# Retention and maxout FFN in fp32: the first FFN products by a bilinear algorithm of rank 20

## The chip, the cores and the metric

The kernel runs on one core of one Trainium2 chip. The time is the device time in microseconds; of the kernel before it was taken in three runs, and the median counts. A core has a matrix engine (TensorE, in the profile PE, with its weight loads as a row of their own, PEld), a vector engine (VectorE, DVE), a scalar engine (ScalarE, ACT), GpSimd (POOL) and the queue that starts the DMA transfers (SyncE, SPq). TensorE writes its results to PSUM, which this kernel uses as eight banks; VectorE and ScalarE read them from there. Each engine works through its own list of instructions, and semaphores make one wait for another.

## What is computed

```python
def _attn_ref(q, k, v):                       # 8 batches, 8 heads, 576 positions, 64 per head
    scores = scale * np.matmul(q, k.transpose(0, 1, 3, 2))
    ...
    ret = scores * Dmat[None, :, :, :]        # causal, with a decay per head
    return np.matmul(ret, v)

def _moe_ref(x, w1, w2, w3, w_out):           # x: 4608 tokens x 512, w1..w3: 512 x 768, w_out: 768 x 512
    h = np.maximum(np.maximum(x @ w1, x @ w2), x @ w3)
    return (h @ w_out).astype(np.float32)
```

The output of the attention, with the heads side by side, is the x of the FFN. Everything is in fp32.

## The kernel before

The tokens are worked off in nine tiles of 512 (t = 0 to 8). For each tile the FFN computes the three products with w1, w2, w3 and their maximum h ("up"), and then the product with w_out ("down"). Between the parts of a tile's FFN stand the steps of the attention for the next tile: transposes, scores, masks, states and values; the last of them (`output`) writes the next tile's x. Tile 0 runs plain products, since the weights are still being converted to fp32 then. From tile 1 on, both products are done by a scheme for 2x2 blocks that needs seven block products instead of eight, and sums of blocks ahead and behind.

The pools that matter, and the inputs' sums at the end of `output`:

```python
C = 128; NT = 4 * C; NH = NT // 2
...
    ps_r = ctx.enter_context(tc.tile_pool(name="ps_r", bufs=4, space=PSUM))
    ps_x = ctx.enter_context(tc.tile_pool(name="ps_x", bufs=2, space=PSUM))
    ps_y = ctx.enter_context(tc.tile_pool(name="ps_y", bufs=2, space=PSUM))
...
    def output(chunks, o, t, i):
        ...                                   # xT[t] <- o * decay, on VectorE
        if i == CPT - 1 and t > 0:
            ...
            nc.vector.tensor_tensor(s1[:], a21, a22, op=ALU.add)
            nc.vector.tensor_tensor(s2[:], s1[:], a11, op=ALU.subtract)
            nc.gpsimd.tensor_tensor(s3[:], a11, a21, op=ALU.subtract)
            nc.gpsimd.tensor_tensor(s4[:], a12, s2[:], op=ALU.subtract)
```

One unit of "up" makes two blocks of 128 features of one of the three products; a tile has nine units. A product is two matmuls of 128x128 weights by 256 tokens. Here x, y and z are PSUM banks, and `kept` copies one to SBUF on ScalarE while the chain goes on:

```python
    def up(t, h, fp, i):
        ...
        product(1, x, True)
        p1 = kept("p1", x)
        chore()
        yield
        y = ps_y.tile([P, NH], FP32, tag="y", name="y")
        product(2, y, True)
        nc.vector.tensor_tensor(c11, y[:], p1[:], op=ALU.add)
        yield
        product(6, x, False)
        u2 = kept("u2", x)
        ...
        product(7, z, True)
        p7 = kept("p7", z)
        yield
        product(5, x, False)
        nc.vector.tensor_tensor(c22, x[:], p7[:], op=ALU.add)
        ...
        product(4, z, False)
        nc.vector.tensor_tensor(c21, z[:], u2[:], op=ALU.add)
        if i > 0:
            nc.vector.tensor_tensor(h[:, f1, hi], h[:, f1, hi], c22, op=ALU.max)
        ...
        product(3, x, False)
        ...                                   # two more maxima into h
```

"Down" has seven products of six matmuls each, in the order 1, 2, 6, 7, 5, 4, 3. The step `values` of the attention, and with it `output`, stands between product 7 and product 5:

```python
        product(5, x, False)
        total(1, 1, x, p7)                    # VectorE reads x; product 3 goes into the same bank
        yield
        product(4, z, False)
        total(1, 0, z, u2)
        yield
        ...
            product(3, x, False, blocks)
```

The FFN of a tile and the attention of the next are interleaved so:

```python
    def steps(t):
        ...
        for n in range(0, CPT, 2):
            a, b, m = CPT * t + n, CPT * t + n + 1, 6 * (n // 2)
            at(m, (keep, a), (transposes, a), (load, a + 2))
            at(m + 1, (transposes, b), (decay_values, b))
            at(m + 2, (scores, a), (scores, b), (load, b + 2))
            at(m + 4, (decay_values, a + 2))
            at(m + 5, (values, [a, b], [b, a + 2]))
        return todo

    for t in range(N // NT):
        work = ffn(t)
        for todo in steps(t + 1):
            for step in todo:
                step()
            next(work, None)                  # nine parts of up, then three of down
```

Of the kernel before, what the change touches and what calls it, by code (L numbers as in the profile page):

```python
# [33 lines left out]
FP32 = mybir.dt.float32  # L35
# [7 lines left out]
C = 128  # L43
NT = 4 * C
# [3 lines left out]
FILL = 224  # L48
WAHEAD = 6
# [3 lines left out]
def kernel(  # L53
# [32 lines left out]
    spool = ctx.enter_context(tc.tile_pool(name="spool", bufs=1))  # L86
# [5 lines left out]
    wtmp = while_converting.enter_context(tc.tile_pool(name="wtmp", bufs=4))  # L92
    ps_r = ctx.enter_context(tc.tile_pool(name="ps_r", bufs=4, space=PSUM))
# [28 lines left out]
    def warm_quarters(n):  # L122
        ps = [ps_y.tile([P, P // 2], FP32, tag="y", name="warm") for _ in range(2)]
        for _ in range(n):
            for r in range(2):
                rows = ident[P // 2 * r:P // 2 * (r + 1), :P // 2]
                for c in range(2):
                    nc.tensor.matmul(ps[r][P // 2 * c:P // 2 * (c + 1), :], lhsT=rows, rhs=rows, start=True, stop=True)

# [23 lines left out]
    def load_blocks(g, *blocks):  # L153
        for n, src in (("q", q), ("kx", k)):

            if 0 in blocks:
                raws[n, g] = raw.tile([P, NP, C // 32, 32], FP32, tag=n, name=n + "raw", bufs=3 if n == "q" else 2)
            t = raws[n, g]
            for blk in blocks:
                b, pos = divmod(g * C + 32 * blk, S)  # L160
                for a in range(4):
                    nc.sync.dma_start(
                        t[32 * a:32 * a + 32, :, blk, :],
                        src[b, a // 2::2, pos:pos + 32, 32 * (a % 2):32 * (a % 2) + 32].rearrange("p j i -> j p i"))

    def load(g):
        if g >= BY_PE and ("q", g) not in raws:
            load_blocks(g, *range(C // 32))
        for n, src in (("k", k), ("q", q), ("v", v)) if g < BY_PE else (("k", k), ("v", v)):
            t = raws[n, g] = raw.tile([C, H, D], FP32, tag=n, name=n + "raw", bufs=4 if n == "k" else 3)  # L170
# [110 lines left out]
    def output(chunks, o, t, i):  # L281
# [8 lines left out]
        if i == CPT - 1 and t > 0:  # L290
            x = xT[t]
            a11, a12, a21, a22 = (x[:, 2 * d:2 * d + 2, NH * r:NH * (r + 1)] for r in range(2) for d in range(2))
            s1, s2, s3, s4 = (spool.tile([P, 2, NH], FP32, tag=f"S{n}", name=f"S{n}") for n in (1, 2, 3, 4))
            nc.vector.tensor_tensor(s1[:], a21, a22, op=ALU.add)
            nc.vector.tensor_tensor(s2[:], s1[:], a11, op=ALU.subtract)
            nc.gpsimd.tensor_tensor(s3[:], a11, a21, op=ALU.subtract)
            nc.gpsimd.tensor_tensor(s4[:], a12, s2[:], op=ALU.subtract)
            xS[t] = {1: a11, 2: a12, 3: s4[:], 4: a22, 5: s1[:], 6: s2[:], 7: s3[:]}
# [13 lines left out]
    w_sb, wT, bits, to_load = {}, {}, {}, deque(pieces)  # L312
# [16 lines left out]
    late, chores = {}, deque()  # L329

    def chore(n=1):
        for _ in range(min(n, len(chores))):
            chores.popleft()()
# [21 lines left out]
    def sums_of_hidden(h, fp):  # L355
# [3 lines left out]
        chores.append(lambda: vec(s1, a21, a22, op=ALU.add))  # L359
        chores.append(lambda: vec(s2, s1, a11, op=ALU.subtract))  # L360
        chores.append(lambda: (pool(s3, a11, a21, op=ALU.subtract), pool(s4, a12, s2, op=ALU.subtract)))  # L361

    def downs(t, h):
# [7 lines left out]
        NM = NH // P  # L371
        last = t == N // NT - 1
# [3 lines left out]
        def bank(pool, tag, name):  # L376
            b = pool.tile([P, NM, DM // 2], FP32, tag=tag, name=name)
            return [b[:, m, :] for m in range(NM)]
# [8 lines left out]
        def kept(name, src):  # L387
            both = []
            for m in range(NM):
                c = ppool.tile([P, NH], FP32, tag=name, name=name)  # L390
                nc.scalar.copy(c[:], src[m])
                both.append(c)
            return both
# [5 lines left out]
        def total(r, c, src, others):  # L399
            osb = opool.tile([P, NM, DM // 2], FP32, tag="osb", name="osb")  # L400
            for m, o in enumerate(others):
                nc.vector.tensor_tensor(osb[:, m, :], src[m], o[:], op=ALU.add)
# [7 lines left out]
        p1 = kept("p1", x)  # L410
# [6 lines left out]
        u2 = kept("u2", x)  # L417
# [3 lines left out]
        p7 = kept("p7", z)  # L421
# [15 lines left out]
    def convert_all():  # L437
# [23 lines left out]
        def product(piece, high, expo, mant):  # L461
# [5 lines left out]
            else:  # L467
                w = w_sb[piece] = const.tile([P, DM], FP32, name=f"w{i}_{fb}")[:]
# [13 lines left out]
    def weight_sums(n):  # L482
        if n >= len(units):
            return
        fp, i = units[n]
        half = [slice(0, DM // 2), slice(DM // 2, DM)]
        b11, b21 = (w_sb[i, 2 * fp][:, r] for r in half)
        b12, b22 = (w_sb[i, 2 * fp + 1][:, r] for r in half)
        t1, t2, t4 = (late["pool"].tile([P, DM // 2], FP32, name=f"T{m}_{i}_{fp}")[:] for m in (1, 2, 4))
        nc.vector.tensor_tensor(t1, b12, b11, op=ALU.subtract)  # L490
        nc.vector.tensor_tensor(t2, b22, t1, op=ALU.subtract)
        nc.gpsimd.tensor_tensor(b12, b22, b12, op=ALU.subtract)
        nc.gpsimd.tensor_tensor(t4, b21, t2, op=ALU.subtract)
        wT[fp, i] = {1: b11, 2: b21, 3: b22, 4: t4, 5: t1, 6: t2, 7: b12}
# [7 lines left out]
    def up(t, h, fp, i):  # L502

        f0, f1, lo, hi = 2 * fp, 2 * fp + 1, slice(0, NH), slice(NH, NT)
        x = ps_x.tile([P, NH], FP32, tag="x", name="x")
        y = {}

        def product(n, out, first):
            w = wT[fp, i][n]
            for d in range(2):  # L510
                nc.tensor.matmul(out[:], lhsT=w[:, d * P:(d + 1) * P], rhs=xS[t][n][:, d, :],  # L511
                                 start=first and d == 0, stop=d == 1, skip_group_check=True)

        def kept(name, src):
            c = ppool.tile([P, NH], FP32, tag=name, name=name)
            nc.scalar.copy(c[:], src[:])  # L516
            return c

        if i == 0:
            c11, c21, c22 = h[:, f0, lo], h[:, f0, hi], h[:, f1, hi]  # L520
        else:
            tmp = ppool.tile([P, 3, NH], FP32, tag="tmp", name="tmp", bufs=1)
            c11, c21, c22 = (tmp[:, n, :] for n in range(3))
        product(1, x, True)
        p1 = kept("p1", x)
        chore()
        yield
        y = ps_y.tile([P, NH], FP32, tag="y", name="y")
        product(2, y, True)
        nc.vector.tensor_tensor(c11, y[:], p1[:], op=ALU.add)  # L530
        yield
        product(6, x, False)
        u2 = kept("u2", x)
        chore()
        yield
        z = ps_y.tile([P, NH], FP32, tag="y", name="z")
        product(7, z, True)
        p7 = kept("p7", z)
        yield
        product(5, x, False)  # L540
        nc.vector.tensor_tensor(c22, x[:], p7[:], op=ALU.add)  # L541
        chore()
        yield
        product(4, z, False)
        nc.vector.tensor_tensor(c21, z[:], u2[:], op=ALU.add)
        if i > 0:
            nc.vector.tensor_tensor(h[:, f1, hi], h[:, f1, hi], c22, op=ALU.max)
        yield
        product(3, x, False)
        if i == 0:  # L550
            nc.scalar.copy(h[:, f1, lo], x[:])
        else:
# [203 lines left out]
```

## Time and profile before

| what | value |
|---|---|
| median of three runs | 797.98 us (796.83 to 798.51) |
| span of the profiled run | 796.0 us |
| TensorE, matmul | 785.0 us busy, 5172 instructions |
| VectorE | 417.6 us busy, 833 instructions |
| ScalarE | 174.4 us busy, 402 instructions |
| GpSimd | 139.9 us busy, 158 instructions |
| granted TensorE clock | 1.00 of full speed |

The page of the profile gives for each engine the time in which it worked, then the span in slices, the chain of work that ended last, and groups of instructions by line, engine and shape. One fp32 matmul leaves two records of the matrix engine and two weight loads; so "x4" in a row of the timeline is two matmuls. The ends of matmuls are modelled, so their starts are the better measure. In a row of the timeline stand the start, the duration, the engine, the line, the operation, what it writes and reads, and how long the engine was idle before it and what released it.

By the starts of the "up" matmuls in the timeline, a tile in mid-kernel takes some 85 us: tile 3 from 296.6 to 381.7 us.

### The profile page before, as it was taken

Reading aid. Unit: us, or ns where it says so; the run is one execution under the profiler, and the core shown is the slowest. Engines: PE = TensorE matmul, PEld = TensorE weight load, DVE = VectorE, ACT = ScalarE, POOL = GpSimd, SP = SyncE. Lnnn points to the kernel's source line nnn. Section 1 sums busy time; section 2 is a strip of 40 time slices with the busy share of each in tenths; the row PEclk is TensorE's granted clock in tenths of the full one; section 3 lists DMA queues with packets and bytes.
Section 4 is the critical chain, followed back from the end, with each engine's and each line's share of the span. In section 5 each row is a group of like instructions: output and inputs, shape, how many; then the busy total and the mean of one; then the engine's idle time right before and its main releaser. Section 6 shows DMA issues by size and latency. Waiting matters only on the chain.

```text
span 796.0 us, 13774 instructions
## 1 busy us (share of the span) xinstructions
PE 785.0 (99%) x5172; PEld 643.0 (81%) x5172; DVE 417.6 (52%) x833; ACT 174.4 (22%) x402; POOL 139.9 (18%) x158
## 2 busy tenths in 40 slices
PE   8899999999999999999999999999999999999998
PEld 7445456888888888888888888888888888888887
DVE  2898979664454534364535354544545343642441
ACT  2664632111111111111111111111111111112111
POOL 3110108511210130112111121112111201110000
DMA  9995643333333323332233423333333332001001
GB/s 212 233 230 127 173 91 100 57 55 57 89 58 57 58 75 61 64 58 60 63 56 55 89 59 57 57 57 90 58 55 57 78 68 54 1 14 40 1 1 53
DMA packets 236930, 59.27 MB, mean 74 GB/s; under 512 B 217920, under 2 KB 235584, under 8 KB 236864
## 3 DMA queue, kind: packets, MB, share of 16 engines
q1 hardware_dynamic: 236432, 58.14, 33.9%
q8 instruction: 40, 0.66, 0.4%
q10 hardware_dynamic: 432, 0.27, 0.1%
q14 instruction: 26, 0.21, 0.1%
HBM read 48.89 MB, written 9.44 MB: 73 GB/s over the span
## 4 chain that ended last, share of the span: by engine, by line
PE 95%; SPq 2%; DMA 1%; issue 0%; ACT 0%; DVE 0%; ACTq 0%
PE x L511 32%; PE z L511 15%; PE dx L383 11%; PE up L573 8%; PE y L511 8%; PE dz L383 5%; PE s L204 4%; PE o L257 4%; PE dy L383 3%; PE down L562 2%; PE o L270 2%; PE kv L224 2%; SPq L172 1%; DMA kraw<-in_k_dram 1%; SPq L327 0%; DMA out_dram<-osb 0%
## 5 line engine op out<-in xcount | busy, mean ns | idle before, releaser
L511 PE MATMUL x<-S,T 128*128 128x256 f32 x576 | 148.0, 379 | 0.6 <-ACT p L516 0.6
L511 PEld LDWEIGHTS x<-S,T 128*128 128x128 f32 x576 | 109.0, 190 | 16.4 <-ACT p L516 1.0
L361 POOL TENSOR_TENSOR H<-h 128x256 f32<-128x256 f32 x24 | 21.0, 873 | 320.9 <-DVE h L554 320.9
L511 PE MATMUL x<-xT,w 128*128 128x256 f32 x288 | 76.1, 387 | 0.0
L511 PE MATMUL x<-S,w 128*128 128x256 f32 x288 | 74.4, 381 | 0.7 <-DVE h L541 0.7
L511 PE MATMUL z<-xT,T 128*128 128x256 f32 x288 | 73.9, 379 | 0.0
L511 PE MATMUL y<-xT,w 128*128 128x256 f32 x288 | 73.9, 379 | 0.0
L511 PE MATMUL z<-S,w 128*128 128x256 f32 x288 | 73.9, 379 | 0.0
L541 DVE TENSOR_TENSOR tmp<-x,p 128x256 f32<-128x256 f32 x48 | 20.4, 425 | 100.2 <-PE x L511 100.2
L516 ACT COPY p<-x 128x256 f32<-128x256 f32 x72 | 26.8, 372 | 192.1 <-PE x L511 192.1
L286 DVE TENSOR_TENSOR xT<-o,gq 128x512 f32<-128x512 f32 (+1 forms) x40 | 23.6, 633 | 84.6 <-PE o L270 84.6
L573 PE MATMUL up<-xT,w 128*128 128x512 f32 x144 | 63.5, 596 | 0.5 <-DVE xT L286 0.5
L511 PEld LDWEIGHTS x<-S,w 128*128 128x128 f32 x288 | 49.4, 189 | 14.2 <-issue 1.3
L511 PEld LDWEIGHTS z<-S,w 128*128 128x128 f32 x288 | 54.7, 190 | 7.4
L511 PEld LDWEIGHTS y<-xT,w 128*128 128x128 f32 x288 | 54.7, 190 | 7.4
L511 PEld LDWEIGHTS x<-xT,w 128*128 128x128 f32 x288 | 53.0, 190 | 9.6 <-issue 1.5
L511 PEld LDWEIGHTS z<-xT,T 128*128 128x128 f32 x288 | 54.2, 189 | 7.9
L573 PEld LDWEIGHTS up<-xT,w 128*128 128x128 f32 x144 | 26.8, 190 | 32.3 <-issue 29.8
L207 DVE TENSOR_TENSOR st<-s,causal 128x512 f32<-128x512 f32 x72 | 45.0, 684 | 11.6 <-PE s L204 10.7
L176 POOL TENSOR_TENSOR vd<-vraw,gk 128x512 f32<-128x512 f32 x36 | 38.8, 1077 | 62.1 <-DMA vraw<-in_v_dram 62.1
L516 ACT COPY u<-x 128x256 f32<-128x256 f32 x72 | 26.8, 372 | 100.1 <-PE x L511 91.7
L383 PE MATMUL dx<-To,H 128*128 128x256 f32 x192 | 44.8, 383 | 0.0
(95 smaller groups left out, 1061.8 us busy)
## 6 DMA issues: line engine op xcount, KB each, us to landing
bits<-in_moe_w_dram SPq DMA_DIRECT2D x36, 256.0 KB, 5.1
out_dram<-osb SPq DMA_DIRECT2D x35, 256.0 KB, 2.1
kraw<-in_k_dram SPq DMA_DIRECT2D x32, 256.0 KB, 3.0
vraw<-in_v_dram SPq DMA_DIRECT2D x32, 256.0 KB, 3.5
qraw<-in_q_dram SPq DMA_DIRECT2D x464, 16.0 KB, 1.8
kxraw<-in_k_dram SPq DMA_DIRECT2D x464, 16.0 KB, 1.8
bits<-in_moe_w_out_dram SPq DMA_DIRECT2D x6, 512.0 KB, 4.5
qraw<-in_q_dram SPq DMA_DIRECT2D x6, 256.0 KB, 4.9
```

Source lines behind the costliest of these rows:

```text
L176: nc.gpsimd.tensor_tensor(t[:], raws.pop(("v", g))[:], gk[:].unsqueeze(2).to_broadcast([C, H, D]), op=ALU.mult)
L204: nc.tensor.matmul(s[j][:, p, :], lhsT=kT[r, p, :], rhs=qT[r, p, :], start=True, stop=True)
L207: nc.vector.tensor_tensor(st[:, j], s[j][:], masks[start_of(g)][:].unsqueeze(1).to_broadcast([C, NP, C]), op=ALU.mult)
L224: nc.tensor.matmul(kvs[g][half(h % 2), h // 2, :], lhsT=kr[r:, h, :], rhs=vds[g][r:, h, :], start=True, stop=True)
L257: nc.tensor.matmul(o[n % 2][half(c), m, n // 2, :], lhsT=vds[g][:, h, :], rhs=sts[g][:, h % 2, h // 2, :], start=m == 0 and n < 2, stop=be ...
L286: nc.vector.tensor_tensor(xT[t][:, b::2, i * C:(i + len(chunks)) * C].rearrange("p u (m c) -> p u m c", c=C), o[b][:].rearrange("p m u c - ...
L361: chores.append(lambda: (pool(s3, a11, a21, op=ALU.subtract), pool(s4, a12, s2, op=ALU.subtract)))
L383: nc.tensor.matmul(out[m], lhsT=hS[n](fp)[:, m * P:(m + 1) * P], rhs=late["T"][n][:, fp, :], start=first and fp == 0 and (m == 0 or last a ...
L511: nc.tensor.matmul(out[:], lhsT=w[:, d * P:(d + 1) * P], rhs=xS[t][n][:, d, :], start=first and d == 0, stop=d == 1, skip_group_check=True)
L516: nc.scalar.copy(c[:], src[:])
L541: nc.vector.tensor_tensor(c22, x[:], p7[:], op=ALU.add)
L573: nc.tensor.matmul(ps[:], lhsT=w_sb[i, fb][:, dc * P:(dc + 1) * P], rhs=xT[t][:, dc, :], start=(dc == 0), stop=(dc == NDC - 1))
```

## The change

For one block of 128 features and one tile, the three maxout products together are a product of 2x4 blocks of x (two halves of the tokens, four blocks of 128 of the model width) by 4x3 blocks of weights. Done plainly that is 24 block products. The change does it with 20, each one matmul of 128x128 weights by 256 tokens, with 13 sums over the inputs per tile and 19 sums over the weights, done once. The seven-product scheme of the kernel before needs 21 for the same work (126 per tile for six blocks of features, against 120). The 20 products run in five chains A to E, each in one PSUM bank; a chain is read after some of its products and then goes on adding. A and B take banks of the x pool, C, D and E of the y pool. The six outputs come together on VectorE from these readings. Tile 1 does two of its six triples plainly, with 512 tokens at once, so that the weight sums can be made meanwhile. Down keeps its seven products; its copies and totals now take two blocks in one instruction. All sums over inputs go to VectorE. To make room in SBUF, the loads of q, k and v have fewer buffers after the first tile.

```diff
+X_SUMS = """s3 = a22 - a12, s13 = a12 + a13, s19 = a12 + a14, s15 = s19 - a22, s10 = s3 - a13, s20 = s10 + a23,
+            s14 = a24 - s15, s11 = s20 + a24, s11 = a21 - s11, s7 = s11 - s13, s6 = s19 + s7,
+            s16 = a11 - s11, s16 = s16 - a14"""
+W_SUMS = """b33 = b13 + b33, n1 = b13 + b43, n2 = n1 - b41, n3 = b11 - n2, n4 = b33 - b32, b43 = b43 + n4,
... (19 sums in all)
+PRODUCTS = """C s3 b23, D s7 b43, B s15 n5, A a22 b21, C a13 b31, B s19 b41, A s10 b32, C a11 b11, B s6 n2, A s13 b22,
+              D s16 b13, B s14 n1, A s11 n4, E a11 b12, B a23 n6, A s20 b33, B a21 n3, E a14 b42, A a21 n8, A a24 n7"""
...
-            t = raws[n, g] = raw.tile([C, H, D], FP32, tag=n, name=n + "raw", bufs=4 if n == "k" else 3)
+            bufs = 3 if n == "k" else 2
+            pool, bufs = (raw0, 1) if g < BY_PE and g % (bufs + 1) == bufs else (raw, bufs)
...
     def output(chunks, o, t, i):
...
-            nc.vector.tensor_tensor(s1[:], a21, a22, op=ALU.add)
-            nc.vector.tensor_tensor(s2[:], s1[:], a11, op=ALU.subtract)
-            nc.gpsimd.tensor_tensor(s3[:], a11, a21, op=ALU.subtract)
-            nc.gpsimd.tensor_tensor(s4[:], a12, s2[:], op=ALU.subtract)
+            for dst, _, a, sign, b in X_SUMS:
+                combine(*(xS[t][n] for n in (dst, a, b)), sign)
+
+    def combine(dst, a, b, sign):
+        nc.vector.tensor_tensor(dst, a, b, op=ALU.add if sign == "+" else ALU.subtract)
...
-    def up(t, h, fp, i):
+    def up(t, h, fb):
+        lo, hi = h[:, fb, 0:NH], h[:, fb, NH:NT]
+        of_a = ppool.tile([P, 4, NH], FP32, tag="of_a", name="of_a")
+        of_b = ppool.tile([P, 4, NH], FP32, tag="of_b", name="of_b", bufs=1)
+        a1, c1, d1 = (ppool.tile([P, NH], FP32, tag=n, name=n, bufs=1)[:] for n in ("a1", "c1", "d1"))
+        kept = {"C1": c1, "D1": d1, "B1": of_b[:, 1], "A1": a1, "B2": of_b[:, 0], "A2": of_a[:, 0],
+                "B3": of_b[:, 2], "A3": of_a[:, 1], "B4": of_b[:, 3], "A4": of_a[:, 2], "A5": of_a[:, 3]}
...
+        def after(step):
+            if step in kept:
+                nc.scalar.copy(kept[step], ps[step[0]][:])
+            if step == "A3":
+                join(of_a[:, 0:2], of_a[:, 0:2], of_b[:, 0:2])
+                join(of_a[:, 0], ps["C"][:], of_a[:, 0])
+            elif step == "A4":
+                join(of_a[:, 2], of_a[:, 2], of_b[:, 2])
+                join(of_a[:, 1:3], of_a[:, 1:3], c1.unsqueeze(1).to_broadcast([P, 2, NH]))
+                join(of_a[:, 2], ps["D"][:], of_a[:, 2])
+                join(of_a[:, 0], of_a[:, 0], of_a[:, 2], ALU.max)
+            elif step == "B6":
+                join(a1, ps["B"][:], a1)
+                join(of_a[:, 3], of_a[:, 3], of_b[:, 3])
+            elif step == "E2":
+                join(of_a[:, 1], ps["E"][:], of_a[:, 1])
+                join(of_a[:, 3], of_a[:, 3], d1)
+                join(lo, of_a[:, 0], of_a[:, 1], ALU.max)
+            elif step == "A7":
+                join(a1, ps["A"][:], a1, ALU.max)
+                join(hi, a1, of_a[:, 3], ALU.max)
+
+        done = {}
+        for chain, x, w in PRODUCTS:
+            n = done[chain] = done.get(chain, 0) + 1
+            if n == 1:
+                pool, tag = (ps_x, "x") if chain in "AB" else (ps_y, "y")
+                ps[chain] = pool.tile([P, NH], FP32, tag=tag, name=chain.lower())
+            ends = n == sum(c == chain for c, _, _ in PRODUCTS)
+            nc.tensor.matmul(ps[chain][:], lhsT=factor(w, fb), rhs=xS[t][x], start=n == 1, stop=ends,
+                             skip_group_check=True)
+            after(f"{chain}{n}")
+            yield
...
     def ffn(t):
...
+        plain = (2, 3) if t == 1 else ()
+        order = [*plain, *(fb for fb in range(NF) if fb not in plain)]
+        total = sum(24 if fb in plain else len(PRODUCTS) for fb in order)
...
+            for step, cost in enumerate(steps_of_one):
+                if fb in plain:
+                    chore(6)                  # weight sums
+                elif step % 5 == 4:
+                    chore()                   # sums over h for down, when there are any
+                count += cost or 1
+                if count * (NF // 2 * 3) >= (parts + 1) * total:
+                    parts += 1
                     yield                     # nine parts: here the attention's steps come in
```

`join` is an instruction of VectorE. A3 is the third product of chain A, and so on; the other chains' products are counted alike.

## The prediction

> **What bounds the kernel now.** I read the page first, for the engine that fills the span and the chain that ended last:
>
> ```profile
> PE 785.0 (99%) x5172; PEld 643.0 (81%) x5172; DVE 417.6 (52%) x833; ACT 174.4 (22%) x402; POOL 139.9 (18%) x158
> ...
> PE 95%; SPq 2%; DMA 1%; issue 0%; ACT 0%; DVE 0%; ACTq 0%
> ```
>
> TensorE carries the chain. Busy PE time is modelled, so I took its real pace from the starts in the timeline: an FFN stretch of tile 3, and a plain stretch of tile 0.
>
> ```profile
> 347.44 1.03 PE L511 MATMUL x<-S,T 128*128 128x256 f32 x4
> 348.30 1.03 PE L511 MATMUL z<-S,w 128*128 128x256 f32 x4
> 349.16 1.03 PE L511 MATMUL x<-S,T 128*128 128x256 f32 x4
> ...
> 53.41 14.00 PE L573 MATMUL up<-xT,w 128*128 128x512 f32 x32
> ```
>
> A new pair of 256-column matmuls (four records) starts every 0.864 us: 0.432 us each, with no gap. Plain 512-column matmuls take 13.9/16 = 0.87 us, so two halves of 0.432 cost what one whole does. A saved product is worth 0.432 us and no more.
>
> Next, how long an answer of the other engines takes, from the timeline of all engines:
>
> ```profile
> 312.76 1.03 PE L511 MATMUL y<-xT,w 128*128 128x256 f32 x4
> 312.96 0.37 ACT L516 COPY p<-x 128x256 f32<-128x256 f32 x1 [5.21 <-PE x L511]
> 313.63 1.03 PE L511 MATMUL x<-S,T 128*128 128x256 f32 x4
> 313.88 0.42 DVE L530 TENSOR_TENSOR tmp<-y,p 128x256 f32<-128x256 f32 x1 [0.40 <-issue]
> ...
> 132.28 0.41 DVE L541 TENSOR_TENSOR h<-x,p 128x256 f32<-128x256 f32 x1
> 132.75 1.13 PE L511 MATMUL x<-S,w 128*128 128x256 f32 x4 [0.73 <-DVE h L541]
> ```
>
> A reader starts 0.20 to 0.27 us after the next matmul has begun (313.63 to 313.88), a copy takes 0.37, and PE restarts 0.06 after its releaser (132.69 to 132.75), its first record then taking 483 instead of 379 ns: 0.10 more per stall. The spacing of two products between copy and reuse leaves 0.864 - 0.25 - 0.37 - 0.06, under 0.2 us. The kernel has no slack to spare; it just fits.
>
> Last, the seam between tiles, where the next tile's inputs are combined:
>
> ```profile
> 373.86 2.86 PE L383 MATMUL dx<-To,H 128*128 128x256 f32 x12
> 373.96 1.29 DVE L286 TENSOR_TENSOR xT<-o,gq 128x512 f32<-128x512 f32 x2 [7.78 <-PE o L270]
> 375.29 0.69 DVE L294 TENSOR_TENSOR S<-xT 128x512 f32<-128x512 f32 x1
> 376.01 1.64 DVE L295 TENSOR_TENSOR S<-S,xT 128x512 f32<-128x512 f32 x1
> 377.57 0.41 DVE L234 TENSOR_TENSOR state<-kv,state 128x256 f32<-128x256 f32 x1
> 377.91 0.74 DVE L402 TENSOR_TENSOR osb<-dx,p 128x256 f32<-128x256 f32 x2
> 379.14 2.75 PE L383 MATMUL dx<-w_out,H 128*128 128x256 f32 x12
> ```
>
> The second product into dx (373.86) must be read by the add at 377.91 before the third (379.14) may write. VectorE is done at 378.65, half a microsecond early.
>
> [...] The add at 376.01, beside a GpSimd subtraction, took 1.64 us, the one before it 0.69. [...]
>
> **The matmuls saved.** Per tile from 2 to 8, 9 x 7 x 2 = 126 matmuls become 6 x 20 = 120: 6 x 0.432 = 2.6 us, for seven tiles 18.1. Tile 1 has four triples of 20 and two plain ones of 12 x 0.87: 34.6 + 20.9 = 55.5 against 54.4, so +1.1. Tile 1 also had 1.5 us of stalls (0.58 and 0.73 us idle, plus restarts) beside its weight sums; the plain triples give those time. Sum: -18.5 us, 2.3%, if nothing waits.
>
> **Chain E waits for chain C.** The y pool has two banks, C and D take them, and E (place 14 of 20) needs C's. C is read only by the second add after A's third product (place 10). Let 0 be the moment when place 11 may start. The copy of A runs 0.25 to 0.62. VectorE's 512-wide add starts at 0.67; a dependent instruction follows a 512-wide one after 0.72 (375.29 to 376.01), so the add that reads C starts at 1.39 and ends at 1.81. PE may resume at 1.87 and pays 0.10. Places 11 to 13 end at 3 x 0.432 = 1.30. Loss 0.67 us in each triple, 7 x 6 + 4 = 46 times: +31 us.
>
> I walked on from there to look for other such places. PE, restarted at 1.87 + 0.10, ends places 14 to 20 at 2.40, 2.84, 3.27, 3.70, 4.13, 4.57 and 5.00. VectorE starts the joins of A's fourth product at 1.97, 2.43, 3.15 (this one reads D, until 3.57) and 3.61, those of B at 3.97 and 4.30, those of E at 4.64 (E is read by 5.06), 4.97 and 5.31, the last two at 5.65 (A is read by 6.07) and 6.11. The next triple's C starts at 5.00, its D, which needs E's bank, at 5.43, its A, which needs the old A's, at 6.29: 0.2 to 0.4 us to spare. Between a copy and the reuse of its bank there are two products everywhere, as before. So one place waits while nothing else is in VectorE's queue.
>
> **Attention's transposes.** The parts of a tile now fall at 14, 27, 40... products, so twice per tile (first and fifth triple) the two transposes are issued after place 14, in front of the adds that free B, E and A. They take 1.25 us (0.62 start to start). In the clock above they run from 3.95 to 5.20 and push the read of E from 5.06 to 6.29, while the next D wants its bank at 5.43: 0.92 + 0.10, then A gets its own 0.15 late. 1.2 us x 2 x 6 tiles = 14, plus 0.8 in tile 1: +15 us. The last tile has no such work.
>
> **The seam.** The two S sums of 512 on VectorE become 13 of 256. Independent ones start 0.335 apart (309.06 to 309.40), dependent ones 0.45 (129.75 to 130.20); 7 and 6 of these are 5.1 us. From 375.29 that ends at 380.4, the state add at 380.7, the add that frees dx (now one of 512) at 381.4, and PE resumes at 381.5 instead of 379.14, plus restart: 2.4 us, at seven seams (the one after tile 0 has no such chain): +17 us.
>
> **Beside other work.** ScalarE gets 66 copies per tile instead of 30, some 13 us more in 85; VectorE 78 joins, about 6 x 5.5 = 33 us instead of 20, plus 3 or 4 for the inputs: from 41 (the table of busy times by stretches, tile 3) to some 57 us in 85. Neither is full. The 57 weight sums, about 21 us of VectorE, lie under tile 1's plain triples. Fewer GpSimd sums help; those of hidden, still in mid-triple, may slow joins: +2 us.
>
> Sum: 798 - 18.5 + 31 + 15 + 17 + 2 = 844. The delays are counted as if none hid another, so I say 838.
>
> **The rivals.** (1) All waits fit and the saving arrives: 780. For it: an engine at 99% busy, 18 us of products gone, VectorE only two thirds full. Against it: the slack under 0.2 us, and two joins in series before E. (2) VectorE's total becomes the bound: then about 57 us of work plus queueing would have to exceed 88 us; the sums are against it. Order, not load, hurts; were queueing much worse, 870. (3) Only the seam and half of the E wait come true: 798 - 18.5 + 17 + 15 = 812. (4) Input loads late, as q, k and v have a buffer less: the profile shows that stores already tie the DMA queue to each tile's end, and loads end well ahead. I give it nothing.
>
> **Range and chances.** The seam is the surest term, E's wait next, the transposes least, since one late stall shifts the following. Without the transposes and with 0.45 for E I get 798 - 18.5 + 17 + 21 = 818; with every term a quarter larger 860. I take 808 to 860. Faster by 2% needs nearly all three waits absent: 0.07. Within 2%: 0.12. Slower: 0.81.
>
> **What would show it.** In the changed profile: PE matmuls of e with idle time released by VectorE's join of C, about 0.6 us, in nearly every triple; idle before d behind the join of E, after the transposes; some 2.2 us before the last dx products, released by the osb add, with 13 short adds ahead of it; a tile of some 91 us instead of 85. If PE shows 0.432 us starts right through a triple, or E sits in a free bank, the main term is wrong and the time is near 780 to 805.

## The result, and the profile after

| | median, us | range | ratio to before (95% interval) |
|---|---|---|---|
| before | 797.62 | 796.83 to 798.51 | |
| changed | 872.33 | 868.9 to 872.79 | 1.0927 (1.0896 to 1.0958) |

The change costs 75 us, 9%. It was predicted slower, at 838 us with a range up to 860: right in direction, and too small by 34 us.

The page of the changed kernel, first the row of busy times, then the chain that ended last:

```profile
PE 802.7 (92%) x5000; PEld 621.7 (71%) x5000; DVE 560.5 (64%) x1179; ACT 272.2 (31%) x649; POOL 103.4 (12%) x124
...
PE 60%; DVE 24%; SPq 7%; DMA 4%; issue 2%; ACT 2%; DVEq 0%; ACTq 0%
```

TensorE has 172 records less to do (44 of them are warm-up matmuls at the start, of which the changed kernel has fewer) and is busy 92% instead of 99%. VectorE, at 64%, is far from full, yet it carries 24% of the chain, where it carried nothing. That points to an order that hurts, not to a load; runs 4 and 5 below show it.

Some names for what follows: a triple is the work on one block of 128 features, for all three maxout products; a place is one of its 20 products. L581 is the line of these products, by their chains, and L550 that of the joins. L400 is the line of down's matmuls; dx, dy and dz are their PSUM banks. L423 is the add that empties such a bank into osb, the output buffer in SBUF.

The waits of TensorE in the changed kernel (what waited, what released it; us in total, times, longest):

```profile
PE e L581 <- DVE of_a L550: 20.4, 45, 0.8
PE dx L400 <- DVE osb L423: 14.8, 7, 2.2
PE d L581 <- DVE of_a L550: 13.3, 13, 1.7
PE a L581 <- DVE a L550: 3.5, 4, 1.4
PE c L581 <- DVE w L310: 3.4, 1, 3.4
PE d L581 <- DVE h L605: 2.1, 1, 2.1
```

E waits in practically every one of the 46 triples, dx at seven seams, D and A at some of the triples' borders. Before, TensorE waited so in the FFN three times in all, 0.5 to 0.7 us each.

The busy times by stretches, for tiles 1 and 3 of the changed kernel (length of the stretch, then PE, PEld, DVE, ACT and POOL with their instructions, the granted clock, the DMA share and GB/s):

```profile
125.65:228.82 103.17, 91.63 (x533) 66.57 (x532) 76.93 (x167) 20.49 (x51) 17.31 (x20) 0.97 0.27 56
...
323.59:415.55 91.96, 85.14 (x550) 70.05 (x549) 56.93 (x123) 26.83 (x71) 10.32 (x12) 1.00 0.29 58
```

The same tiles took 86.41 and 84.15 us before (tile 3 from 297.58 to 381.73 us; the 296.6 and 85 us given further up are off by a microsecond). VectorE's 57 us and ScalarE's 27 us in tile 3 are what was worked out (57 and some 13 more). The granted clock is 0.97 in tile 1, and 0.98 in tiles 2, 5 and 6; before it was 1.00. Nothing in the prediction had foreseen that.

From the starts of the matmuls I took, for each product, how much later than 0.432 us it began after the one before it, and sorted these excesses by place. With 0.10 us of restart for each wait:

| what | predicted, us | in the trace, us |
|---|---|---|
| products saved, old stalls gone | -18.5 | -18.5 (not measured apart here) |
| E waits for C, 46 times | +31 | 27.9 + 4.6 = 32.5 |
| the seam, 7 times | +17 | 15.9 + 0.7 = 16.6 |
| D and A wait at triples' borders | +15, and +2 for GpSimd | 27.5, with restarts some 31 |
| chain C in tile 1 waits for a weight sum | 0 | 3.6 |
| matmuls at half their pace | 0 | 8.3 |
| sum | 844, then lowered to 838 | 798 + 73.5 = 871.5 |

The profiled spans differ by 75.1 us (796.0 and 871.1), so 1.6 us are not placed. That leaves little for the parts of the change that were not tried alone, such as the wider copies and totals of down.

**E.** The timeline of a first triple of tile 3:

```profile
328.77 0.59 PE L581 MATMUL a<-s,n 128*128 128x256 f32 x2
329.31 0.42 DVE L550 TENSOR_TENSOR of_a<-c,of_a 128x256 f32<-128x256 f32 x1
329.79 0.70 PE L581 MATMUL e<-xT,w 128*128 128x256 f32 x2 [0.42 <-DVE of_a L550]
...
332.50 0.67 DVE L200 STREAM_TRANSPOSE qT<-qraw 128x512 f32<-128x512 f32 x1
...
333.72 0.41 DVE L550 TENSOR_TENSOR of_a<-e,of_a 128x256 f32<-128x256 f32 x1
334.19 0.48 PE L581 MATMUL d<-s,w 128*128 128x256 f32 x1 [0.68 <-DVE of_a L550]
```

E's first product starts 0.06 us after the join that read C ends (329.73), 1.02 us after the product before it: 0.59 more than 0.432. The idle time of 0.42 that the view shows is smaller, since the modelled end of a matmul lies past the start of the next. Further down the transposes stand ahead of the join that reads E, and D, which takes E's bank, starts 0.84 us late.

**The fifth triple.** The same tile, 45 us on:

```profile
374.90 0.42 DVE L374 TENSOR_TENSOR H<-H,h 128x256 f32<-128x256 f32 x1
375.39 0.84 POOL L375 TENSOR_TENSOR H<-h,H 128x256 f32<-128x256 f32 x1 [11.37 <-DVE H L374]
375.68 1.10 DVE L550 TENSOR_TENSOR of_a<-of_a,c 128x512 f32<-128x512 f32 x1
...
380.05 0.70 PE L581 MATMUL d<-s,w 128*128 128x256 f32 x2 [1.29 <-DVE of_a L550]
```

Here D is 1.46 us late. A sum over hidden (H) has come in front of the joins, and GpSimd's subtraction, which that sum releases, runs beside the 512-wide join, which takes 1.10 us instead of 0.69, 0.41 us more. The join ends 0.55 us after the subtraction does (376.78 and 376.23). All 21 joins of 512 columns that begin while GpSimd is at work in this trace end 0.55 us after GpSimd's instruction, and take 0.92 to 1.10 us; the 71 others take 0.69. Three osb adds that began beside GpSimd took 0.68 us all the same; they have one input in PSUM. At the seam of the kernel before it was alike:

```profile
375.33 1.77 POOL L296 TENSOR_TENSOR S<-xT 128x512 f32<-128x512 f32 x1 [10.99 <-DVE xT L286]
```

The S add of 1.64 us, at 376.01, ended 0.55 us after this subtraction (377.65 and 377.10). The one at 375.29 ran beside it too, but had begun first, and took 0.69. So what GpSimd cost these 512-wide adds of two SBUF inputs, which began after it, is the rest of GpSimd's own instruction, less 0.14 us (0.69 - 0.55).

**The seam and what follows it,** in tiles 2 and 3:

```profile
319.21 4.54 PE L400 MATMUL dx<-w_out,H 128*128 128x256 f32 x12 [2.17 <-DVE osb L423]
...
411.78 0.42 DVE L247 TENSOR_TENSOR state<-kv,state 128x256 f32<-128x256 f32 x1
412.12 0.68 DVE L423 TENSOR_TENSOR osb<-dx,of_b 128x512 f32<-128x512 f32 x1
412.85 2.86 PE L400 MATMUL dx<-w_out,H 128*128 128x256 f32 x12 [2.16 <-DVE osb L423]
```

The state add and the osb add, behind the 13 sums, stand in the order that was walked through, and product 3 waits for them at both seams. But six matmuls of the same shape take 2.86 us at one and 4.54 at the other. In tile 1 it is plainer:

```profile
180.78 1.19 PE L581 MATMUL c<-xT,w 128*128 128x256 f32 x2 [3.37 <-DVE w L310]
181.76 1.06 PE L581 MATMUL b<-s,w 128*128 128x256 f32 x2
```

After 3.37 us without work the starts lie 0.85 us apart instead of 0.43, for seven products, and the granted clock stands at 0.50 for 6.83 us (180.06 to 186.89). At the seam dx is 1.68 us longer, and 1.68/0.432 = 3.9 matmuls at half pace, or 3.4 us. There 2.2 us without work went ahead. The same 2.2 us were followed by half pace at three of the seven seams (319, 599 and 694 us) and not at three others; the last seam, with 1.83 us, was spared too. The granted clock in the trace tells them apart. All its changes lie a whole number of 3.413 us apart, so I cut the span at such distances from them and call the pieces windows. At the first of these seams the idle time, from 317.05 to 319.21 us, lies wholly inside one window; in the next one the clock is halved (length, then the engines' busy times as above; the clock is the third value from the right):

```profile
316.60:320.01 3.41, 1.24 (x7) 0.77 (x6) 3.34 (x9) 0.00 (x0) 0.73 (x1) 1.00 0.04 9
320.01:323.42 3.41, 3.41 (x10) 2.70 (x9) 1.29 (x3) 0.00 (x0) 1.73 (x2) 0.50 0.44 154
```

So it is at the other two. At the four seams that were spared an edge between windows cuts the idle time, and at most 1.7 us of it lie in one window. From 100 to 869 us, four windows at full clock in this trace have 2.16 to 2.71 us of idle time, as the view counts it, and each is followed by one at half clock; no other has more than 1.83 us, and none of these others is. Which seams are hit here thus goes with where they fall in these windows. In run 3 below four of the first six seams are hit, in run 8 two: dx takes 4.18 to 4.54 us there and 2.86 at the others of the six, after a wait of 2.15 or 2.16 us at each.

### The profile page after: what moved, and what is told of

Read it like the earlier page. It is cut to its first block, busy times and chain, and to the rows that moved or that the text cites. A ratio compares the mean times of both kernels' runs of the same rounds, so it can differ in the third digit from the quotient of the medians.

```text
span 871.1 us, 13846 instructions
## 1 busy us (share of the span) xinstructions
PE 802.7 (92%) x5000; PEld 621.7 (71%) x5000; DVE 560.5 (64%) x1179; ACT 272.2 (31%) x649; POOL 103.4 (12%) x124
## 4 chain that ended last, share of the span: by engine, by line
PE 60%; DVE 24%; SPq 7%; DMA 4%; issue 2%; ACT 2%; DVEq 0%; ACTq 0%
DVE of_a L550 12%; PE up L602 9%; PE a L581 8%; PE dx L400 8%; PE b L581 7%; SPq L173 6%; PE c L581 4%; PE s L217 4%; PE o L270 4%; DVE s L310 4%; DMA qraw<-in_q_dram 3%; PE dz L400 3%; PE down L591 2%; PE dy L400 2%; PE d L581 2%
## 5 line engine op out<-in xcount | busy, mean ns | idle before, releaser
L550 DVE TENSOR_TENSOR of_a<-of_a,of_b 128x512 f32<-128x512 f32 x138 | 73.3, 531 | 103.4 <-ACT of_a L554 101.6
L554 ACT COPY of_b<-b 128x256 f32<-128x256 f32 x184 | 68.6, 373 | 130.1 <-PE b L581 126.8
L554 ACT COPY of_a<-a 128x256 f32<-128x256 f32 x184 | 68.5, 372 | 86.4 <-PE a L581 78.3
L581 PE MATMUL a<-s,w 128*128 128x256 f32 x276 | 83.1, 383 | 0.0
L581 PE MATMUL b<-s,n 128*128 128x256 f32 x276 | 82.6, 381 | 0.0
L581 PE MATMUL e<-xT,w 128*128 128x256 f32 x184 | 59.5, 405 | 20.4 <-DVE of_a L550 20.4
L581 PE MATMUL d<-s,w 128*128 128x256 f32 x184 | 58.1, 397 | 16.3 <-DVE of_a L550 13.3
L581 PE MATMUL c<-xT,w 128*128 128x256 f32 x184 | 57.8, 396 | 3.4 <-DVE w L310 3.4
L581 PEld LDWEIGHTS e<-xT,w 128*128 128x128 f32 x184 | 31.2, 189 | 41.3 <-DVE of_a L550 38.9
L581 PEld LDWEIGHTS a<-s,w 128*128 128x128 f32 x276 | 52.9, 192 | 7.5
L581 PEld LDWEIGHTS b<-s,n 128*128 128x128 f32 x276 | 52.9, 192 | 7.4
L581 PEld LDWEIGHTS d<-s,w 128*128 128x128 f32 x184 | 32.9, 191 | 30.9 <-DVE of_a L550 25.0
L581 PE MATMUL b<-xT,n 128*128 128x256 f32 x184 | 54.7, 379 | 0.0
L581 PE MATMUL a<-xT,n 128*128 128x256 f32 x184 | 47.2, 379 | 0.0
L400 PE MATMUL dx<-To,H 128*128 128x256 f32 x192 | 44.8, 383 | 0.0
```

The source lines that it names most:

```text
L400: nc.tensor.matmul(out[m], lhsT=hS[n](fp)[:, m * P:(m + 1) * P], rhs=late["T"][n][:, fp, :], start=first and fp == 0 and (m == 0 or last a ...
L550: nc.vector.tensor_tensor(out, a, b, op=op)
L554: nc.scalar.copy(kept[step], ps[step[0]][:])
L581: nc.tensor.matmul(ps[chain][:], lhsT=factor(w, fb), rhs=xS[t][x], start=n == 1, stop=ends, skip_group_check=True)
```

## The experiments

Ratios are to the kernel before on the same chip; its median was 797.6 to 798.8 us on the chips used. For the changed kernel the number is 872.33.

**1. Only C's join earlier.** C is complete at place 8; its join is issued there, instead of behind the 512-wide join at place 10.

```diff
-            if step == "A3":
-                join(of_a[:, 0:2], of_a[:, 0:2], of_b[:, 0:2])
+            if step == "C3":
                 join(of_a[:, 0], ps["C"][:], of_a[:, 0])
+            elif step == "A3":
+                join(of_a[:, 0:2], of_a[:, 0:2], of_b[:, 0:2])
```

> One edit: the join that reads chain C is issued when C ends (after place 8), ahead of the 512-wide join. Base is the changed kernel, 872.3 us. If each wait stands alone, as the prediction summed them, the wait before E (0.69 us in 46 triples) goes and nothing else changes: 840 us. If the waits are links of one VectorE queue, the time gained is lost again at the next link: without the stall at E, PE wants E's bank for the next triple's D at 4.75 us (counted from the end of place 10), and VectorE, whose joins of A's fourth product still start at 1.97, has read E only at 5.04. That is 0.35 + 0.10 in each triple, so only 0.24 x 46 = 11 us are won: about 861 us, with idle time moved from E to D.

Measured: 864.06 us (861.38 to 864.87), ratio 1.0809 (1.0785 to 1.0834). TensorE's largest wait in it:

```profile
PE d L582 <- DVE of_a L550: 31.1, 38, 1.8
```

No wait of E is left, and D's has gone from 13.3 to 31.1 us, at 38 places instead of 13. TensorE now reaches the triple's end sooner, while VectorE has the same joins still to do before the one that reads E. It is one queue: 27.9 us of late E's removed gave 8.

**2. Only the seam.** Three of the 13 input sums stay ahead of the osb add; six follow the first total, four the second.

```diff
-                combine(*(xS[t][n] for n in (dst, a, b)), sign)
+                sums_left.append(partial(combine, *(xS[t][n] for n in (dst, a, b)), sign))
+            input_sums(len(X_SUMS) if t == 1 else 3)
...
         total(1, 1, x, p7)
+        input_sums(6)
         yield
         product(4, z, False)
         total(1, 0, z, u2)
+        input_sums(4)
```

> One edit: of the 13 input sums only 3 stand ahead of the add that frees dx, 6 follow that add and 4 the next one (tile 1's stay together). If the order at the seam is the cause, the seven waits of 2.33 + 0.10 us go, 17 us, and with them the slow matmuls behind some of them (1.7 us each at three seams, seen as half pace after the long idle time): 850 to 855 us, and a granted clock nearer to 1.00 than 0.988. If the number of sums is the cause (VectorE's load), they only move: 872 us.

Measured: 848.39 us (847.58 to 852.66), ratio 1.0635 (1.0605 to 1.0665), 24 us less. That is the 16.6 us of the waits and the 5.2 of half pace behind three of them, and a little more.

**3. Only the attention's places.** Parts of a tile may end only after a triple's place 7 or 20, so the transposes no longer stand ahead of the read of E. The other steps of the attention move with them.

```diff
-                if count * (NF // 2 * 3) >= (parts + 1) * total:
+                if count * (NF // 2 * 3) >= (parts + 1) * total and (fb in plain or step + 1 in (7, 20)):
```

> One edit: the attention steps come in only after place 7 or 20 of a triple, so the transposes never stand between place 14 and the joins of B, E and A. If the transposes hold up the reads of E and A, the waits of 0.84 and 1.46 us (+0.10 each) per tile go for tiles 2 to 7, and about as much in tile 1: some 15 us, 857 us. If they only fill gaps in VectorE's queue: 870 to 873 us.

Measured: 855.56 us (854.25 to 857.35), ratio 1.0715 (1.0694 to 1.0737). The excesses of D and A fall from 27.5 to some 9 us: with the transposes out of the way, D is still 0.2 to 0.5 us late at a time, mostly behind the triples that have a sum over hidden in VectorE's queue and GpSimd at work beside it. The transposes are a cause, and one worth more than the 15 us given to them. The time fell by 17 us only, since the weight sum that C waits for in tile 1 came 1.8 us later still, and four seams instead of three were followed by half pace.

**4. The three edits together.** VectorE runs the same instructions as in the changed kernel, in another order.

> The three edits together; VectorE has exactly the same instructions as in the changed kernel. Sum of the three under the theory of one queue: the seam 17 + 5 of slow clock, the transposes 15, and of the wait at E 11: 824 us, with a wait of some 0.45 us at D left in each triple (21 us) and tile 1's own waits (about 11). If the waits were independent: 803 us. If VectorE's load (560 us busy) were the bound, no reordering would bring more than a few us: over 860 us.

Measured: 828.44 us (828.3 to 833.24), ratio 1.0389 (1.0358 to 1.042). The single edits gave 8, 24 and 17 us, together they give 44. The seam no longer shows among the waits; what is left is mostly D behind its join (16.3 us, 38 times, at most 0.8), then the product of C in tile 1 that waits for a weight sum (5.1 us) and other products of C behind a join (4.3 us, 13 times). VectorE's load is the same, and the time is 44 us less: the order is the cause of these.

**5. The joins rebuilt.** Each bank is read as soon as its chain is complete, with the sums not yet needed moved behind, and one instruction more per triple.

```diff
-            if step == "A3":
+            if step == "C3":
+                join(of_a[:, 0], ps["C"][:], of_a[:, 0])
+            elif step == "B3":
+                join(of_b[:, 2], of_b[:, 2], c1)
+            elif step == "D2":
+                join(of_b[:, 2], ps["D"][:], of_b[:, 2])
                 join(of_a[:, 0:2], of_a[:, 0:2], of_b[:, 0:2])
-                join(of_a[:, 0], ps["C"][:], of_a[:, 0])
+                join(of_a[:, 1], of_a[:, 1], c1)
             elif step == "A4":
                 join(of_a[:, 2], of_a[:, 2], of_b[:, 2])
-                join(of_a[:, 1:3], of_a[:, 1:3], c1.unsqueeze(1).to_broadcast([P, 2, NH]))
-                join(of_a[:, 2], ps["D"][:], of_a[:, 2])
                 join(of_a[:, 0], of_a[:, 0], of_a[:, 2], ALU.max)
```

> The joins of a triple issued as their parts come in: C when it ends, C1 and then D added to B's third reading before A's fourth product is there (one 512-wide join less, two 256-wide more; one more instruction in each triple). Seam, places and tile 1 as in the changed kernel. By the clock counted from the end of place 10: after A's fourth product only one add and one maximum stand before the joins of B and E; E is read by 4.38, D wants its bank at 4.75, A is read by 5.39 and wanted at 5.62. If the length of the queue between a read and its successors is the cause, the wait at E goes (32 us) and does not come back at D; the transposes still cost about 0.65 and 1.2 us per tile. Expected 832 us, no waits at E, and triples without attention at 0.432 us per product. If the wait moves on to the next bank again, as when C alone was read earlier: 860 us.

Measured: 831.41 us (830.2 to 834.12), ratio 1.0421 (1.0394 to 1.0447). 41 us of the 75 lie in the order of six joins, one of which was split in two. E's wait is gone without reappearing at D, which from tile 2 on is late behind transposes (mostly 0.47 us in the first and 1.07 in the fifth triple) and only twice elsewhere by more than 0.2 us (0.64 and 0.66).

**6. Only tile 1.** Four plain triples instead of two, and the weight sums spread thinner over them, in another order.

```diff
-            weight_sums(2)
             weight_sums(1)
-        plain = (2, 3) if t == 1 else ()
+            weight_sums(2)
+        plain = (2, 3, 5, 4) if t == 1 else ()
...
-                    chore(6)
+                    chore(4 if n < 2 else 3)
```

> Tile 1 does four of its six triples plainly (two more, 1.8 us each by the products), with the sums over the weights spread over twelve plain steps instead of six and those for the last features last; the rest as in the changed kernel. If the crowding of the 57 weight sums caused the waits of tile 1 (2.3 us at D, 1.6 at A, 3.6 at C, and some 3 us of half pace after it), tile 1 falls from 103 us to about 90 and the kernel to 858 us. If these waits came from something else (loads, or the joins themselves), more plain triples only add: 874 us.

Measured: 864.79 us (861.05 to 865.95), ratio 1.0825 (1.0799 to 1.085). Tile 1 goes from 103.17 to 93.85 us, although two more plain triples cost 2 x 1.8 us of products. The wait for the weight sum and the half pace after it are gone. Of these 9.3 us the time shows 7.5: tile 1 began 3.3 us later in this profile.

**7. The loads' buffers.** The kernel before, with the changed kernel's smaller buffers for q, k and v.

```diff
-            t = raws[n, g] = raw.tile([C, H, D], FP32, tag=n, name=n + "raw", bufs=4 if n == "k" else 3)
+            bufs = 3 if n == "k" else 2
+            pool, bufs = (raw0, 1) if g < BY_PE and g % (bufs + 1) == bufs else (raw, bufs)
+            t = raws[n, g] = pool.tile([C, H, D], FP32, tag=n, name=n + "raw", bufs=bufs)
...                                           # the pool raw0, and two buffers for q loaded in blocks
```

> The kernel before, with one part of the change alone: q, k and v have the buffers of the changed kernel (one less each after the first tile). If the loads still come in time, 798 us, within 0.5%. If late loads are part of the loss, as the longer waits of GpSimd for v could suggest: 803 us or more.

Measured: 799.01 us (797.71 to 800.2), ratio 1.0009 (0.9999 to 1.0019). The smaller buffers by themselves cost next to nothing. In the changed kernel's trace, too, TensorE waits for a load only in the first 25 us. Late loads are not part of the loss.

**8. Only the sums over hidden.** They are issued at a triple's first four places, where VectorE is idle.

```diff
-                elif step % 5 == 4:
+                elif step < 4:
                     chore()
```

> The changed kernel, with one edit: the sums over hidden (two on VectorE and GpSimd's subtractions) are issued at the first four places of a triple, where VectorE is idle, instead of at every fifth place. Theory, that these sums standing in VectorE's queue among the joins, and GpSimd's subtraction running beside the 512-wide join, are what made the waits of D and A larger than predicted: the 0.23 us waits after the third triples vanish and the D wait of the fifth triple goes from 1.46 us to some 0.85; about 1.1 us in each of seven tiles, 872 to some 864 us. Rival, that the transposes and E's wait alone make them: 870 to 873 us, and the fifth triple's D keeps waiting about 1.4 us.

Measured: 861.12 us (859.33 to 861.34), ratio 1.078 (1.0765 to 1.0796). The late starts of 0.23 us behind the third triples are gone, the fifth triple's D is 0.71 or 0.72 us late in five of six tiles (1.09 in one) instead of 1.46, and the first triple's is unchanged at 0.84: what remains is about the size that transposes alone make. All excesses of D and A fell from 27.5 to 15.2 us. In exchange those of E rose from 27.9 to 32.7. One seam fewer was followed by half pace, which is 1.7 of the 11 us. One place where E waits the longer:

```profile
368.80 1.04 POOL L189 TENSOR_TENSOR vd<-vraw,gk 128x512 f32<-128x512 f32 x1
369.09 1.30 DVE L550 TENSOR_TENSOR of_a<-of_a,of_b 128x512 f32<-128x512 f32 x1 [1.12 <-ACT of_a L554]
370.98 0.70 PE L581 MATMUL e<-xT,w 128*128 128x256 f32 x2 [1.03 <-DVE of_a L550]
```

The decay of the values on GpSimd, in its queue behind the subtraction, now falls beside the first 512-wide join, which ends 0.55 us after it, takes 1.30 us, and holds up E. The hidden sums' own time on VectorE and GpSimd's slowing of a join were not told apart by this run; the lines of the fifth triple show both.

**9. The edits of runs 5, 2, 3 and 6 together.**

> Rebuilt joins, split seam, moved places and tile 1 with four plain triples. The products save 18.1 us in tiles 2 to 8 and cost 4.7 in tile 1, the old stalls of tile 1 (1.5 us) go: 798.8 - 18.1 + 4.7 - 1.5 = 784 us if nothing waits. With some waits left where GpSimd works beside the joins, about 3 us: 787 us, 1.5% faster than the kernel before. If VectorE's load of about two thirds makes waits of its own whatever the order: 800 us or more.

Measured: 800.06 us (797.77 to 804.54), ratio 1.0027 (1.0016 to 1.0039). A miss by 13 us: no faster than before. In the profile (of a run of 804.54 us, the slowest) D was still late behind hidden sums and joins (6.1 us, 13 times), behind the last input sum at tile starts (3.6 us, 4 times, one of 2.1), and after that one half-pace matmuls came again (starts 0.85 us apart).

**10. The same, with the hidden sums at places 1 to 4, the input sums split 5, 6 and 2, and no weight sums in the later down products of tile 1.**

```diff
-            input_sums(len(X_SUMS) if t == 1 else 3)
+            input_sums(len(X_SUMS) if t == 1 else 5)
...
-        input_sums(4)
+        input_sums(2)
...
-                    chore(4 if n < 2 else 3)
-                elif step % 5 == 4:
+                    chore(5 if n < 2 else 3)
+                elif step < 4:
                     chore()
...
         for n, _ in enumerate(downs(t, h)):
-            chore(2)
+            chore((4, 4, 4, 2, 0, 0, 0)[n])
```

> The kernel with the joins rebuilt, the seam split, the attention's steps moved and tile 1 with four plain triples, in which now the sums over hidden are issued at a triple's first four places, five input sums stand before the seam, six after the first total and two after the second, and no weight sums are left for the later down products of tile 1. Theory, that what was left above the sum of its products (some 13 us) were the D waits behind the hidden sums, the last input sum and tile 2's weight sums: those waits go and it takes 783 to 787 us. Rival, that other waits take their place, or the start is the difference: 797 us or more.

Measured: 793.09 us (791.82 to 793.83), ratio 0.9931 (0.9917 to 0.9944). Faster than before by 0.7%, but 6 us short of what was expected. The waits named were gone and another had come. The timeline at the end of its tile 5:

```profile
546.97 6.29 SPq L425 DMA_DIRECT2D out_dram<-osb  x4
...
551.55 0.69 DVE L430 TENSOR_TENSOR osb<-dz,of_a 128x512 f32<-128x512 f32 x1 [2.91 <-DMA out_dram<-osb]
...
552.30 0.70 PE L593 MATMUL d<-s,w 128*128 128x256 f32 x2 [1.82 <-DVE osb L430]
```

VectorE is ready but idle for 2.91 us: of the two osb buffers none is free, since the stores are only then going out (SyncE issues four of them between 546.97 and 553.26 us). D needs the bank that this add reads.

**11. The same as 10, with the warm-up matmuls of the kernel before** (four and six rounds of quarters, for six).

```diff
-    warm(6)
+    warm(4)
+    warm_quarters(6)
...                                           # and the function warm_quarters
```

> The same kernel with the warm-up matmuls of the kernel before (four large ones and six rounds of quarters, instead of six large ones). Theory, that the later start of tile 1 seen in some profiles (129 us instead of 126) comes with the shorter warm-up: up to 3 us less than without, 782 to 785. Rival, that the start varies by itself: the same within 1 us.

Measured: 794.05 us (791.01 to 797.15), ratio 0.9953 (0.9937 to 0.997). The warm-up is not what shifts the start. Some 2 of the 3 us are TensorE's clock: in the traces of runs 5, 6 and 9 it falls to half between 23 and 25 us and stays there for some 10 us, the first eight matmuls of up take 9.05 to 9.18 us, against 7.13 in runs 3 and 8, and tile 0 takes 99.0 to 99.1 us. In the changed kernel and in runs 3, 4, 8 and 10 to 12 it takes 97.1. Why the clock does so in some of them stays open.

**12. The same as 10, with three osb buffers.**

```diff
-    opool = ctx.enter_context(tc.tile_pool(name="opool", bufs=2))
+    opool = ctx.enter_context(tc.tile_pool(name="opool", bufs=3))
```

> The kernel of the second round of repairs, with one edit: three output buffers osb instead of two. Theory, that its last waits (D behind the osb add, 5.5 us at five tile starts with up to 2.2 each, and some 2 us of restarts and half-pace matmuls after the longest) come from that add finding both osb buffers still being stored, behind the loads in SyncE's queue: they go, and it takes 784 to 787 us, against 793. Rival, that the add is late through VectorE's own queue: 791 to 794, the waits stay.

Measured: 786.28 us (785.35 to 786.73), ratio 0.9841 (0.9827 to 0.9855). Its row of busy times, its chain, and tile 3 in the busy times by stretches:

```profile
PE 774.2 (99%) x4968; PEld 617.4 (79%) x4968; DVE 543.3 (69%) x1201; ACT 264.2 (34%) x629; POOL 99.2 (13%) x124
...
PE 93%; DVE 3%; DMA 2%; SPq 1%; issue 0%; ACT 0%; DVEq 0%; ACTq 0%
...
298.42:379.97 81.55, 81.55 (x549) 71.19 (x548) 55.84 (x130) 26.60 (x71) 10.06 (x12) 1.00 0.33 65
```

Tile 3 takes 81.55 us, against 84.15 before: 2.60 us less, which is 6 x 0.432. In this tile the saved products arrive in full; tiles 2 to 8 together are 13.4 us shorter than before, of the 18.1. This version beats both kernels, by 1.6% and by 10%. Of the 18.1 us that the products are worth, the longer tile 1 takes 2.7 back (89.14 against 86.41), short waits of A for ScalarE's last osb copy (2.1 us idle, 2.6 with what follows) and smaller ones some more.

## Why the prediction was wrong in size

Three steps failed. The term for the transposes and the hidden sums was given 17 us and measured 31. The weight sums, said to lie under tile 1's plain triples, held up TensorE there (3.6 us at C, and some of the waits at D that are in the 31). And the sum had no place for matmuls at half their pace after long waits (8.3 us), while 6 us were taken off for delays that were to hide one another. The main mechanism, E waiting for the join that reads C, was right. The steps one by one:

- **"A saved product is worth 0.432 us and no more", -18.5.** Right for the product: it can only be seen once the waits are gone (2.60 us in tile 3 of run 12). The whole sum was not measured for this kernel, and even run 12 keeps 13.4 of the 18.1 us.
- **"Chain E waits for chain C", 0.67 in each triple.** Right in place, cause and size: mostly 0.59 and a restart of 0.10, in all 46 triples. Runs 1 and 5 confirm the join of C in VectorE's queue as the cause. Run 1 also shows that "so one place waits" holds only for this order: the slack of 0.2 to 0.4 us that was left at D is too small to take anything up.
- **"The seam", 2.4 at seven places.** Right: 2.33 and 0.10; run 2.
- **"Attention's transposes", 1.2 x 2 x 6 + 0.8 = 15, with 2 for the hidden sums.** The mechanism was right, and this is the term that was most mis-sized: some 31 us. The first triples are as worked out (0.84 and 0.10, against 0.92 and 0.10). The fifth were taken to be alike and are 1.46, or 1.83 once. The walk through VectorE's queue never put the sums over hidden into it, though the diff issues them at every fifth place, in the middle of the joins; and the line of 1.64 us beside a GpSimd subtraction had been read, but priced with 2 us for the whole kernel. It was also read by halves: the add ahead of it ran beside the same subtraction and kept its 0.69 us, as it had begun first. Run 8 takes 11 us away with the place of the hidden sums alone, 1.7 of them by one half-paced seam fewer. Smaller waits of the same kind (0.2 us at D after most third triples, 0.2 to 1.2 at A) make up some more, and 5.6 us lie in tile 1.
- **"The 57 weight sums ... lie under tile 1's plain triples."** False. They were weighed against the tile, and not against the moment when each is needed: 3.6 us at one product of C, and 4 us at D (counted in the 31 above), partly behind the plain triple's own maximum, which stands behind weight sums in the queue. Run 6: 9.3 us less in this tile, in spite of two more plain triples.
- **Restart at 0.10 us per stall.** Right for a short wait. After four of the long ones (2.2 us at three seams, 3.4 in tile 1) the matmuls run at half pace for some 3 us or more: 5.2 us at the three seams and 3.1 in tile 1, that had no place in the sum.
- **"Counted as if none hid another, so I say 838."** Wrong direction. The waits lie one behind the other on TensorE's path, and nothing hid another. With the measured sizes in place of the worked-out ones: 844 + 14 (D and A) + 3.6 + 8.3 + 1.5 (E) - 0.4 (the seam) = 871.
- **Rivals.** The load of VectorE (2) is refuted by run 5, which has one join more per triple and takes 41 us less; late loads (4) by run 7, rightly given nothing. Rival 1, that the saving arrives, needs what run 12 has. Rival 3, half of the E wait, did not come true: E waited in all 46 triples.

## What to carry to other kernels

Here an engine at 99% gained from fewer instructions only once the banks, sums and buffers came free in time (872.33 us with the change alone, 786.28 in run 12). So walk every instruction of the engine that frees them through its queue, the rare ones too (transposes, sums for later stages, a slower neighbour on GpSimd), and do not take a discount for delays that lie in series on the bounding engine. Where an order hurts and not a load, read each PSUM bank right when its chain ends and put the sums that nobody waits for behind (41 us in run 5). When a repair gives less than the wait it removed, list the waits again: three times here the gain was held up by the next in line, last of all by an output buffer.

## What was not expected of the hardware

- Matmuls ran at half pace for about 3.4 us after 2.2 us without work, at three of the seven seams: those where the idle time lay inside one of the windows of 3.413 us at whose edges this trace's granted clock changed. After 3.4 us without work, 2.65 of them in one window, it was two windows, seven products.
- A 512-wide add of two SBUF inputs took 0.69 us alone. Begun while GpSimd was at work it ended 0.55 us after GpSimd's instruction: 1.10 us beside a subtraction of 256, 1.30 beside a multiplication of 512, 1.64 in the kernel before.
